# Three edits in a fused attention and token-MLP kernel: own buffers for the last residual, earlier operand sums, merged steps

## Chip, core and metric

The kernel runs on one core of one Trainium2 chip. The metric is device time of one execution in microseconds (us), lower is better. Engines are called PE (TensorE, matrix products), PEld (its weight loads), DVE (VectorE), ACT (ScalarE), POOL (GpSimd) and SP (SyncE, which here only issues transfers).

## What is computed

One block on x of 2048 tokens x 512 channels, in float32. First h = x + A(layernorm(x)), where A is a linear attention with 32 heads. Then

```
n = layernorm(layernorm(h))            # 2048 x 512
u = gelu(n^T @ w1 + b1)                # 512 x 1792, over the tokens
out = h + (u @ w2 + b2)^T              # 2048 x 512
```

The change lies in the second half, the two products with w1 (2048 x 1792) and w2 (1792 x 2048), which mix tokens.

## The kernel before

**Precision and products.** Every float32 operand is split into a high part (a copy rounded to the matmul's type, by ACT) and a low part (operand minus high part, by DVE or POOL), and a product is high x high + high x low + low x high: three matmuls. Both token products are done mostly by blocks of 2 x 2 tiles with seven block products instead of eight. That takes sums of tiles on both sides before the products, seven operands each, and sums of the seven results behind them. A tile is 128 x 128 on the weight's side and 128 x 256 (HD = 256 channels) on the other.

**w1 stage.** The 14 column tiles of w1 make 7 pairs p = 0 to 6. Pairs 0, 1, 2 and 6 are "plain pairs" (`fill`, or `seven_step` for the rest of pair 2): twelve matmuls of 512 columns for each two token tiles and pair of columns. Pairs 3, 4, 5 (`SEVEN`) go by seven products: 21 matmuls of 256 columns a step (L933). `RUN` lists the steps of the loop at L980: n = 0 to 5 are the last six steps of pair 2, n = 6 to 13 those of pair 3, 14 to 21 of pair 4, 22 to 29 of pair 5. In step n PE does the step, DVE makes the low part of step n + 1 (L912, or L914 in pair 2), a load is issued, DVE makes the weight sums of step n + 3 (L888 and L890, pairs 3 to 5 only) and ACT its high part (L894, or L884). The rings hold four raw tiles, three high and three low parts. `early` puts the gelu of pairs 0 and 1 and the last operand parts of h (`t_lo`, L647) into steps 0, 1 and 3. `seven_out` (L937) turns the seven results of a pair into u: it takes two places a step in the pair that follows. When pair p is done, `U[p]` holds gelu of its four tiles.

**Operands of u.** For the second product each pair needs three sums beside its four tiles, in a tile `tt`, and high and low parts of all seven. `near_ops` does it for pairs 0 and 1 into their own tiles `un`: the four sums on POOL (L807 to L810), the high parts on ACT (L816, L817), the low parts on DVE (L818, L819). Both pairs' `tt` come from the pool `ut`, which has one buffer. `near_ops(0)` is written into step 8 and `near_ops(1)` into step 16; their ACT and DVE parts follow two to five steps later through the lists `late` and `heavy`. `operands_u` (L821) does the same for pairs 2 to 6, the sums on DVE (L824 to L827) and the parts into `uf` tiles (ACT L61, DVE L62); there `tt` comes from `h7` for odd pairs and from `ut` for even ones. The buffer of `h7` first holds `hb7`, a part of h, whose last reader is `t_lo(7)` in step 3.

**w2 stage.** The steps are (sp, p), for eight token pairs sp and seven p; the weights come in groups of two steps (GRP = 2): load on SP (L1048), sums on DVE (L854 to L856), high part on ACT (L1066), low part on DVE (L1076). The first p of a token pair goes through `products`, the last two (last three for sp = 7) too, all at once. Those between go through `step`: five products as "wide" matmuls of 512 columns with the high weights (high and low of u side by side), then five of 256 columns with the low weights (L1104), then two products as six "narrow" ones (L1108). For sp = 7 all seven products are narrow, nine matmuls each for its last three p together, 63 in all. Behind each token pair DVE builds two output tiles in `ot` (one buffer, L1182 and `out_block`), and POOL's queue adds them to `out` in memory, which already holds h (L1169, L1175 to L1177). For the last token pair h is loaded instead (L1185, SP) into the same `ot`, b2 is added (L1186), and the results are added in place as the banks complete (L1187 to L1198): bank 0 after 18 of the 63 matmuls, bank 1 after 36, bank 2 after 54, bank 3 after the last. Three stores end the kernel (L1196, L1199).

**Order.** Inside `manual_schedule` the named engines take the instructions in the order of the text. What is outside (`operands_u`, the rest of pair 6, all of SP) is placed by the planner, which simulates the program and puts instructions where its simulation finds the engine free; it may put them between those of a manual order.

Of the kernel before, what the change touches and what calls it, by code (L numbers as in the profile page):

```python
# [9 lines left out]
F32 = mybir.dt.float32  # L10
# [7 lines left out]
P = 128  # L18
# [4 lines left out]
NP = NF // 2  # L23
HD = D // 2
GRP = 2
NG = 8
SEVEN = (3, 4, 5)
# [11 lines left out]
def block_kernel(ctx: ExitStack, tc: tile.TileContext, x, xT, wT, phic, wo, w1, b1, w2, b2,  # L39
# [753 lines left out]
    NEAR = 2  # L793
# [3 lines left out]
    def gelu(f, pu):  # L797
        if f % 2 == 0:
            U[f // 2] = ur.tile([P, 4, HD], F32, name="u")
        nc.scalar.activation(U[f // 2][:, f % 2 * 2:f % 2 * 2 + 2].rearrange("p k d -> p (k d)"), pu,  # L800
                             AF.Gelu_apprx_tanh, bias=b1s[:, f:f + 1])

    def near_ops(p):

        u = U[p]
        tt = ut.tile([P, 3, HD], F32, name="tt")
        nc.gpsimd.tensor_sub(tt[:, 0], u[:, 0], u[:, 1])  # L807
        nc.gpsimd.tensor_sub(u[:, 0], u[:, 2], u[:, 0])
        nc.gpsimd.tensor_sub(tt[:, 1], u[:, 2], tt[:, 0])
        nc.gpsimd.tensor_sub(tt[:, 2], u[:, 3], tt[:, 1])  # L810
        parts = [near[p][:, 0:4], near[p][:, 4:7]]
        for m in range(7):
            UB[p, m] = near[p][:, m]

        def high():
            nc.scalar.activation(parts[0][:, :, 0], u, AF.Copy)  # L816
            nc.scalar.activation(parts[1][:, :, 0], tt, AF.Copy)  # L817
        return [high, lambda: nc.vector.tensor_sub(parts[0][:, :, 1], u, parts[0][:, :, 0]),  # L818
                lambda: nc.vector.tensor_sub(parts[1][:, :, 1], tt, parts[1][:, :, 0])]  # L819

    def operands_u(p):  # L821
        u = U[p]
        tt = h7.tile([P, 3, HD], F32, name="tt", tag="h7") if p % 2 else ut.tile([P, 3, HD], F32, name="tt")
        nc.vector.tensor_sub(tt[:, 0], u[:, 0], u[:, 1])  # L824
        nc.vector.tensor_sub(u[:, 0], u[:, 2], u[:, 0])
        nc.vector.tensor_sub(tt[:, 1], u[:, 2], tt[:, 0])
        nc.vector.tensor_sub(tt[:, 2], u[:, 3], tt[:, 1])  # L827
        m = 0
        while m < 7:
            at = (p - NEAR) * 7 + m  # L830
            n = 2 if at % 2 == 0 and m not in (3, 6) else 1
            if at % 2 == 0:
                far[at // 2] = big.tile([P, 2, 2, HD], F32R, name="uf", tag="big")
            part = far[at // 2][:, at % 2:at % 2 + n]
            src = u[:, m:m + n] if m < 4 else tt[:, m - 4:m - 4 + n]
            split(part[:, :, 0], part[:, :, 1], src, nc.vector)
            for k in range(n):
                UB[p, m + k] = part[:, k]
            m += n
# [136 lines left out]
        return [lambda c=c: gelu(2 * p + c, PU[p][c]) for c in range(2)]  # L976

    early = {0: [*seven, *gelus(0)], 1: [lambda: t_lo(6), lambda: t_hi(7), *gelus(1)], 3: [lambda: t_lo(7)]}
    todo, heavy, late = [], [], []
    for n, (p, i) in enumerate(RUN):  # L980
        if n == NT // 2 - AHEAD:
            ms.close()
            ms.enter_context(tc.manual_schedule(engines={ET.PE, ET.DVE, ET.Activation, ET.Pool}))
        seven_step(p, i)
        seven_lo()
        seven_load()
        for op in early.get(n, []):
            op()
        if n == NT // 2 - AHEAD:
            for op in gelus(2):  # L990
                op()
        sum_with(*todo[:2])
        todo = todo[2:]
        if heavy:
            op = heavy.pop(0)
            op and op()
        if i == 1 and p > SEVEN[0]:
            todo += seven_out(p - 1)
        if i == 2 and 0 <= p - SEVEN[0] < NEAR:
            late = near_ops(p - SEVEN[0])  # L1000
        if i == 4 and late:
            late.pop(0)()
            heavy += [late[0], None, late[1]]
            late = []
    wst.close()
    hp = ctx.enter_context(tc.tile_pool(name="hp", bufs=1, reuse_waits="tile"))
    wst = ExitStack()
# [93 lines left out]
    def wide(sp, p, a, b, bk, low):  # L1101
        w, u = AW[sp, p][low][:, a], UB[p, b]
        o, u = (bank[bk][:, 0], u[:, 0]) if low else (bank[bk], u)
        nc.tensor.matmul(o, w, u, start=p == 0 and not low, stop=p == NP - 1, skip_group_check=True)  # L1104
# [3 lines left out]
            nc.tensor.matmul(bank[bk][:, half], AW[sp, p][x][:, a], UB[p, b][:, y], start=p == 0 and half == 0 and i == 0,  # L1108
                             stop=p == NP - 1 and i == 2, skip_group_check=True)

    def step(sp, p, order):
        for low in range(2):
            for a, b, bk, half in order:
                if half is None:
                    wide(sp, p, a, b, bk, low)
        for a, b, bk, half in order:
            if half is not None:
                narrow(sp, p, a, b, bk, half)

    def flat(a):  # L1120
        return a.rearrange("p k d -> p (k d)")
# [3 lines left out]
    for n, (sp, p) in enumerate(STEPS):  # L1125
        t = 2 * sp
        last = t + 2 == NT
        if n % GRP == 0 and p < NP - 1:
            lo_w2()
            hi_w2()  # L1130
            sums_w2()
        if p == 0:
            bank = []
            for _ in range(6):
                pool = (ps_f, ps_q, ps_b, ps_b)[n_bank % 8 // 2]
                bank.append(pool.tile([P, 2, HD], F32, name="py", tag="pu"))
                n_bank += 1
        order = LAST if last else PROD
        run_on = 3 if last else 2
        if p == 0:  # L1140
            products(sp, [p], order)
            continue
        if p < NP - run_on:
            step(sp, p, order)
            continue
        if p < NP - 1:
            continue
        products(sp, range(NP - run_on, NP), order)
        e = uo.tile([P, 2, HD], F32, name="e")
        u2 = uo.tile([P, HD], F32, name="u2", bufs=1)  # L1150
        u3 = uo.tile([P, HD], F32, name="u3")
        if not last:
            ot = uo.tile([P, 2, 2, HD], F32, name="ot", bufs=1)
            low = uo.tile([P, 3, HD], F32, name="low")
            nc.scalar.activation(e[:, 1], bank[0][:, 0], AF.Copy)
            for i in range(3):
                nc.scalar.activation(low[:, i], bank[3 + i][:, 1], AF.Copy)
            nc.vector.tensor_add(e[:, 1], bank[0][:, 1], e[:, 1])
            nc.vector.tensor_sub(u2, bank[1][:, 0], e[:, 1])
            nc.vector.tensor_add(u2, bank[1][:, 1], u2)  # L1160
            nc.vector.tensor_sub(u3, u2, bank[2][:, 0])
            nc.vector.scalar_tensor_tensor(e[:, 0], bank[2][:, 1], -1.0, u2, op0=ALU.mult, op1=ALU.subtract)

            def out_block(i, h, o, add):
                nc.vector.scalar_tensor_tensor(ot[:, i, h], o, b2s[:, t + i:t + i + 1], add, op0=ALU.add, op1=ALU.add)  # L1165

            out_block(0, 0, bank[2][:, 1], u3)
            out_block(0, 1, bank[3][:, 0], u3)
            nc.gpsimd.dma_start(out[t * P:(t + 1) * P, :], flat(ot[:, 0]), accum_op=ALU.add)  # L1169
            if n % GRP == 0:  # L1170
                lo_w2()
                hi_w2()
            out_block(1, 0, bank[4][:, 0], e[:, 0])
            out_block(1, 1, bank[5][:, 0], e[:, 1])
            nc.gpsimd.dma_start(out[(t + 1) * P:(t + 2) * P, :], flat(ot[:, 1]), accum_op=ALU.add)  # L1175
            nc.gpsimd.dma_start(out[t * P:(t + 1) * P, HD:D], low[:, 0], accum_op=ALU.add)
            nc.gpsimd.dma_start(out[(t + 1) * P:(t + 2) * P, :], flat(low[:, 1:3]), accum_op=ALU.add)  # L1177
            if n % GRP == 0:
                sums_w2()
            continue  # L1180

        ot = uo.tile([P, 2, 2, HD], F32, name="ot", bufs=1)  # L1182
        hb = [ot[:, i] for i in range(2)]
        for i in range(2):
            nc.sync.dma_start(flat(hb[i]), out[(t + i) * P:(t + i + 1) * P, :])  # L1185
            nc.vector.tensor_scalar(hb[i], hb[i], b2s[:, t + i:t + i + 1], None, op0=ALU.add)  # L1186
        nc.scalar.activation(e[:, 1], bank[0][:, 0], AF.Copy)  # L1187
        nc.vector.tensor_add(hb[1][:, 1], bank[0][:, 0], hb[1][:, 1])  # L1188
        nc.vector.tensor_sub(u2, bank[0][:, 1], e[:, 1])  # L1189
        nc.vector.tensor_sub(hb[1][:, 0], hb[1][:, 0], u2)  # L1190
        nc.vector.tensor_sub(u3, u2, bank[1][:, 0])  # L1191
        nc.vector.tensor_add(hb[0], hb[0], u3.unsqueeze(1).to_broadcast([P, 2, HD]))  # L1192
        nc.vector.tensor_add(hb[0][:, 0], bank[1][:, 1], hb[0][:, 0])  # L1193
        nc.vector.tensor_sub(hb[1][:, 0], hb[1][:, 0], bank[1][:, 1])  # L1194
        nc.vector.tensor_add(hb[0][:, 1], bank[2][:, 0], hb[0][:, 1])  # L1195
        nc.sync.dma_start(out[t * P:(t + 1) * P, :], flat(hb[0]))  # L1196
        for k, o, q in ((0, bank[2][:, 1], nc.scalar), (1, bank[3][:, 0], nc.sync)):
            nc.vector.tensor_add(hb[1][:, k], o, hb[1][:, k])  # L1198
            q.dma_start(out[(t + 1) * P:NT * P, k * HD:(k + 1) * HD], hb[1][:, k])  # L1199
# [49 lines left out]
```

## Time and profile before

| | us |
|---|---|
| median of 3 runs | 521.54 |
| lowest and highest | 521.18, 522.02 |
| profiled execution | 521.74 |
| its span in the profile | 520.0 |

The span runs from the first to the last instruction in the profile; 1.7 us of the profiled execution lie around it. The TensorE clock was granted in full throughout. A row of a timeline gives start and duration in us, engine, line of the kernel, operation, result<-operands, shapes, count, and in brackets the engine's idle time just before and what ended it. Of matmul rows the starts are to be compared: their ends overlap. A row of the windows gives busy time and count of each engine in a stretch. A row of a line's view gives count, durations in ns (lowest, median, highest), and the first and last start.

### The profile page before, as it was taken

Reading aid. Unit: us, or ns where it says so; the run is one execution under the profiler, and the core shown is the slowest. Engines: PE = TensorE matmul, PEld = TensorE weight load, DVE = VectorE, ACT = ScalarE, POOL = GpSimd, SP = SyncE. Lnnn points to the kernel's source line nnn. Section 1 sums busy time; section 2 is a strip of 40 time slices with the busy share of each in tenths; the row PEclk is TensorE's granted clock in tenths of the full one; section 3 lists DMA queues with packets and bytes.
Section 4 is the critical chain, followed back from the end, with each engine's and each line's share of the span. In section 5 each row is a group of like instructions: output and inputs, shape, how many; then the busy total and the mean of one; then the engine's idle time right before and its main releaser. Section 6 shows DMA issues by size and latency. Waiting matters only on the chain. (4 is left out here: it accounts for less than half of the span.)

```text
span 520.0 us, 9480 instructions
## 1 busy us (share of the span) xinstructions
PE 511.8 (98%) x3595; PEld 442.1 (85%) x3595; DVE 445.0 (86%) x789; ACT 296.6 (57%) x494; POOL 245.7 (47%) x188
## 2 busy tenths in 40 slices
PE   8999999999999999999999999999999999999996
PEld 8788888887877767887788999998889999999996
DVE  6893999986899998877787679998999888988984
ACT  6998943524246876668976443556654434434430
POOL 2589799885999999875533003000002112211220
PEclk9999999999999999999999999999999999999999
DMA  8744310000131234343413333346125688667653
GB/s 310 271 139 122 82 42 21 1 1 3 42 123 60 103 84 129 112 128 119 151 50 101 97 88 102 87 123 236 62 88 112 165 184 171 139 151 190 139 71 102
DMA packets 36300, 58.56 MB, mean 113 GB/s; under 512 B 3744, under 2 KB 19360, under 8 KB 36256
## 3 DMA queue, kind: packets, MB, share of 16 engines
q1 hardware_dynamic: 31648, 50.85, 30.6%
q0 software_dynamic: 4032, 6.42, 9.8%
q8 instruction: 28, 0.46, 0.4%
q10 hardware_dynamic: 576, 0.69, 0.4%
q14 instruction: 16, 0.13, 0.1%
HBM read 46.81 MB, written 11.14 MB: 111 GB/s over the span
## 5 line engine op out<-in xcount | busy, mean ns | idle before, releaser
L1066 ACT ACTIVATE whi<-wraw 128x1792 fp32r<-128x1792 f32 x28 | 47.6, 1701 | 42.5 <-DVE wraw L856 21.1
L1076 DVE TENSOR_TENSOR wlo<-wraw,whi 128x1792 fp32r<-128x1792 f32 x28 | 56.6, 2020 | 8.8 <-PE py L1108 7.5
L1169 POOL DMA_DIRECT2D out<-ot x7 | 6.2, 885 | 110.4 <-DVE ot L1165 110.4
L67 PE MATMUL pu<-hs,whi 128*128 128x512 f32 x128 | 50.3, 393 | 1.2 <-POOL hs L62 1.2
L1104 PE MATMUL py<-uf,whi 128*128 128x512 f32 x175 | 50.0, 395 | 0.4 <-DVE uf L62 0.4
L66 PE MATMUL pu<-hs,whi 128*128 128x512 f32 x128 | 50.1, 399 | 0.0
L68 PE MATMUL pu<-hs,wlo 128*128 128x512 f32 x128 | 48.3, 390 | 0.0
L894 ACT ACTIVATE whi<-wraw 128x896 fp32r<-128x896 f32 x24 | 22.9, 953 | 33.8 <-DVE wraw L890 18.6
L456 POOL TENSOR_TENSOR ez<-eq,zB 128x1024 f32<-128x1024 f32 x16 | 38.4, 2400 | 4.4 <-ACT zB L503 4.4
L1108 PE MATMUL py<-uf,whi 128*128 128x256 f32 x210 | 39.0, 283 | 0.0
L933 PE MATMUL pu<-ht,whi 128*128 128x256 f32 x192 | 35.6, 283 | 0.0
L208 POOL TENSOR_TENSOR pk<-pk,sk 128x1024 f32<-128x1024 f32 x16 | 30.9, 1940 | 7.3 <-DVE sk L207 7.2
L62 POOL TENSOR_TENSOR hs<-hb,hs 128x512 fp32r<-128x512 f32 x16 | 22.4, 1400 | 23.9 <-ACT hs L61 23.8
L550 ACT ACTIVATE pht<-tn 128x512 f32<-128x512 f32 x32 | 17.4, 595 | 28.4 <-PE tn L548 28.3
L474 POOL TENSOR_TENSOR eq<-eq,w 128x1024 f32<-128x1024 f32 x16 | 32.4, 2027 | 1.3 <-DVE w L471 1.2
L1108 PEld LDWEIGHTS py<-uf,whi 128*128 128x128 f32 x210 | 32.7, 192 | 0.0
L1104 PEld LDWEIGHTS py<-uf,wlo 128*128 128x128 f32 x175 | 28.5, 189 | 4.9
L1104 PEld LDWEIGHTS py<-uf,whi 128*128 128x128 f32 x175 | 29.2, 189 | 3.4 <-DVE uf L62 0.7
L212 POOL TENSOR_TENSOR zacc<-zacc,pk 128x1024 f32<-128x1024 f32 x13 | 31.3, 2405 | 0.5
L66 PEld LDWEIGHTS pu<-hs,whi 128*128 128x128 f32 x128 | 24.0, 188 | 7.1 <-issue 2.5
L933 PEld LDWEIGHTS pu<-ht,whi 128*128 128x128 f32 x192 | 29.9, 192 | 0.0
L912 DVE TENSOR_TENSOR wlo<-wraw,whi 128x896 fp32r<-128x896 f32 x24 | 26.0, 1085 | 4.5 <-ACT whi L894 4.5
(207 smaller groups left out, 1626.9 us busy)
## 6 DMA issues: line engine op xcount, KB each, us to landing
wraw<-in_w SPq DMA_DIRECT2D x28, 512.0 KB, 4.5
wraw<-in_w SPq DMA_DIRECT2D x48, 256.0 KB, 2.8
xraw<-in_xT SPq DMA_DIRECT2D x16, 256.0 KB, 3.1
xh<-in_x SPq DMA_DIRECT2D x16, 256.0 KB, 2.7
h<-in_x SPq DMA_DIRECT2D x16, 256.0 KB, 2.7
out<-h SPq DMA_DIRECT2D x14, 256.0 KB, 2.9
out<-ot POOLq DMA_DIRECT2D x14, 256.0 KB, 4.9
wraw<-in_wT SPq DMA_DIRECT2D x12, 256.0 KB, 4.9
```

Source lines behind the costliest of these rows:

```text
L66: nc.tensor.matmul(o, ah, bh, start=first, stop=False)
L67: nc.tensor.matmul(o, ah, bl, start=False, stop=False)
L68: nc.tensor.matmul(o, al, bh, start=False, stop=last)
L208: nc.gpsimd.tensor_mul(heads(PK[t]), heads(PK[t]), sk.unsqueeze(2).to_broadcast([P, 2 * H, DH]))
L212: nc.gpsimd.tensor_add(zacc, zacc, PK[t])
L456: nc.gpsimd.tensor_mul(EZ[t], EQ[t], zB)
L474: nc.gpsimd.tensor_mul(heads(EQ[t]), heads(EQ[t]), W[t].rearrange("p g c h -> p (g c h)").unsqueeze(2).to_broadcast([P, 2 * H, DH]))
L933: nc.tensor.matmul(ACC[p][bk][:, half], WS[p, i][x][:, a], hb[b][y], start=i == 0 and half == 0 and k == 0, stop=i == NT // 2 - 1 and k == ...
L1066: nc.scalar.activation(WH[g], RAW[g], AF.Copy)
L1076: nc.vector.tensor_sub(wl_, RAW[g], WH[g])
L1104: nc.tensor.matmul(o, w, u, start=p == 0 and not low, stop=p == NP - 1, skip_group_check=True)
L1108: nc.tensor.matmul(bank[bk][:, half], AW[sp, p][x][:, a], UB[p, b][:, y], start=p == 0 and half == 0 and i == 0, stop=p == NP - 1 and i == ...
```

## The change

Three edits. (1) `near_ops` takes `tt` as `operands_u` does, so pair 1 gets the buffer in `h7`; and its parts move in the loop: the POOL sums of pair 0 to step 1, those of pair 1 to step 4, and the ACT and DVE parts, three for each pair, to steps 2, 3, 4 and 6, 8, 10. (2) `step` becomes `steps`: two steps that use one weight group are done together, the wide high matmuls of both first, then the low and narrow ones of the first, then of the second. (3) For the last token pair the residual gets two tiles of its own, `hb0` and `hb1`, instead of `ot`.

```diff
+    def sums_tile(p):
+        return h7.tile([P, 3, HD], F32, name="tt", tag="h7") if p % 2 else ut.tile([P, 3, HD], F32, name="tt")
...
-        tt = ut.tile([P, 3, HD], F32, name="tt")
+        tt = sums_tile(p)
...
-    todo, heavy, late = [], [], []
+    todo, late = [], []
+    NEAR_AT, LATE_AT = (1, 4), (2, 3, 4, 6, 8, 10)
...
-        if heavy:
-            op = heavy.pop(0)
-            op and op()
         if i == 1 and p > SEVEN[0]:
             todo += seven_out(p - 1)
-        if i == 2 and 0 <= p - SEVEN[0] < NEAR:
-            late = near_ops(p - SEVEN[0])
-        if i == 4 and late:
+        if n in NEAR_AT:
+            late += near_ops(NEAR_AT.index(n))
+        if late and n in LATE_AT:
             late.pop(0)()
-            heavy += [late[0], None, late[1]]
-            late = []
...
-    def step(sp, p, order):
-        for low in range(2):
+    def steps(sp, ps, order):
+        for p in ps:
             for a, b, bk, half in order:
                 if half is None:
-                    wide(sp, p, a, b, bk, low)
-        for a, b, bk, half in order:
-            if half is not None:
-                narrow(sp, p, a, b, bk, half)
+                    wide(sp, p, a, b, bk, 0)
+        for p in ps:
+            for a, b, bk, half in order:
+                if half is None:
+                    wide(sp, p, a, b, bk, 1)
+            for a, b, bk, half in order:
+                if half is not None:
+                    narrow(sp, p, a, b, bk, half)
...
-            step(sp, p, order)
+            if n % GRP == 0 or p == 1:
+                steps(sp, range(p, min(p + GRP - n % GRP, NP - run_on)), order)
...
-        ot = uo.tile([P, 2, 2, HD], F32, name="ot", bufs=1)
-        hb = [ot[:, i] for i in range(2)]
+        hb = [uo.tile([P, 2, HD], F32, name=f"hb{i}", bufs=1) for i in range(2)]
```

More of the change, by code (lines that the diff above doesn't have):

```diff
@@ L822, in operands_u @@
         u = U[p]
-        tt = h7.tile([P, 3, HD], F32, name="tt", tag="h7") if p % 2 else ut.tile([P, 3, HD], F32, name="tt")
+        tt = sums_tile(p)
         nc.vector.tensor_sub(tt[:, 0], u[:, 0], u[:, 1])
```

## Prediction

> **What bounds the kernel now.** I began with the page: its first part says which engine fills the span.
>
> ```profile
> span 520.0 us, 9480 instructions
> PE 511.8 (98%) x3595; PEld 442.1 (85%) x3595; DVE 445.0 (86%) x789; ACT 296.6 (57%) x494; POOL 245.7 (47%) x188
> ```
>
> TensorE is busy for 98% of the span, and the change leaves the number and the shapes of its matmuls alone. So it can only win by closing holes in the PE row, or by shortening the tail that follows the last matmul; and it can lose by opening new ones. I looked for holes in the windows, in the stage whose matmuls are all alike (L933, 256 columns each).
>
> ```profile
> 300.00:320.00 20.00, 20.00 (x169) 20.00 (x168) 17.30 (x30) 9.24 (x11) 4.68 (x4) 1.00 0.33 94
> 320.00:340.00 20.00, 19.49 (x157) 18.73 (x156) 19.84 (x47) 9.71 (x12) 0.00 (x0) 1.00 0.33 93
> ```
>
> Columns: length, then busy us and count of PE, PEld, DVE, ACT and POOL, then the granted clock (1.00 in both). At the same clock the second 20 us hold 12 matmuls fewer, while DVE is busy for 19.84 of 20 with 47 instructions instead of 30. The timeline of PE shows such a hole, the view of line 933 who ended it:
>
> ```profile
> 335.62 0.28 PE L933 MATMUL pu<-hs,wlo 128*128 128x256 f32 x1
> 335.74 0.40 PE L933 MATMUL pu<-hs,whi 128*128 128x256 f32 x2
> 336.43 0.39 PE L933 MATMUL pu<-hs,wlo 128*128 128x256 f32 x1 [0.29 <-DVE wlo L912]
> ```
> ```profile
> L933 PE MATMUL pu<-hs,wlo x72: 283/283/387, 292.4 to 354.0; 128*128 128x256 f32 x72
>   DVE wlo L912: 1.8, 6
> ```
>
> Undisturbed starts lie 0.12 us apart (335.62 to 335.74). The stage has 24 steps of 21 matmuls, 504 in all; that row holds the stage's 3rd matmul (292.4) and its 504th (354.0). 501 x 0.12 = 60.1 us should lie between them; it is 61.6. **About 1.5 us** are lost, where PE waits for the low part of the w1 weights, which DVE makes. After this stage one more hole stands out:
>
> ```profile
> 389.90 0.50 PE L1104 MATMUL py<-uf,whi 128*128 128x512 f32 x1 [0.39 <-DVE uf L62]
> ```
>
> The end I read from the chain that ended last, then from the timelines of PE, ACT, DVE and SP.
>
> ```profile
> 502.91 5.32 DMA out<-ot
> ...
> 508.80 3.41 DMA ot<-out
> ...
> 514.40 0.70 DVE ot L1192
> ...
> 516.54 0.33 DVE ot L1198
> ```
> ```profile
> 509.84 0.28 PE L1108 MATMUL py<-uf,wlo 128*128 128x256 f32 x1
> ...
> 515.24 0.28 PE L1108 MATMUL py<-uf,wlo 128*128 128x256 f32 x1
> 510.16 0.38 ACT L1187 ACTIVATE e<-py 128x256 f32<-128x256 f32 x1 [6.14 <-PE py L1108]
> 516.13 0.74 DVE L1198 TENSOR_TENSOR ot<-py,ot 128x256 f32<-128x256 f32 x2
> 443.29 45.54 SPq L1048 DMA_DIRECT2D wraw<-in_w  x10
> ```
>
> No matmul stands in this chain: the store of the token pair before the last has to leave `ot`, then the residual is loaded into `ot`, then DVE works off its list, until 516.87, though the last matmul started at 515.24.
>
> **Part 1, own buffers for the residual.** The load no longer waits for `ot`. SP has issued its last weight load by 488.8 (443.29 + 45.54), ten in 45 us, so two more issues fit between them or behind them; the 3.4 us load and both L1186 are then over before bank 0 is ready. How soon after its last matmul a bank can be read: the 18th of the last 63 matmuls completes bank 0; it starts at 515.24 - 45 x 0.12 = 509.84, and ACT reads at 510.16, 0.32 later. By the same step bank 1 (36th) is ready at 512.3, bank 2 (54th) at 514.5, bank 3 (63rd) at 515.56. DVE keeps up with that: between banks 1 and 2 stand L1191 to L1194, three of 256 columns (0.34 each, as the chain's 0.33 for L1198) and L1192 with 0.70, 1.7 us of the 2.2; behind bank 2 L1195 and the first L1198, 0.7 us, until 515.2. The last L1198 then runs from 515.56 for 0.41, to 515.97 instead of 516.87: **-0.9 us**. How long the last store takes to land I leave as it is. Ends: 0 (the load still comes late) and -1.3 (the store also lands sooner, since the other two are out of its way; my estimate, no row shows it). I take -0.9, whose rows are this very stretch. What is late next is PE itself.
>
> **Part 2, sums of pairs 0 and 1 in the plain pairs.** The instructions are the same; those of L807 to L819 move from steps 8 to 21 to steps 1 to 10. Before, they lie thus (timelines of POOL, then DVE):
>
> ```profile
> 313.07 1.45 POOL L807 TENSOR_TENSOR tt<-u 128x256 f32<-128x256 f32 x1 [31.66 <-DVE un L819]
> ...
> 316.23 1.68 POOL L810 TENSOR_TENSOR tt<-u,tt 128x256 f32<-128x256 f32 x1
> ```
> ```profile
> 308.00 1.08 DVE L912 TENSOR_TENSOR wlo<-wraw,whi 128x896 fp32r<-128x896 f32 x1
> ...
> 309.98 1.08 DVE L912 TENSOR_TENSOR wlo<-wraw,whi 128x896 fp32r<-128x896 f32 x1
> ...
> 313.85 0.96 DVE L888 TENSOR_TENSOR wraw<-wraw 128x256 f32<-128x256 f32 x1
> 314.84 1.46 DVE L890 TENSOR_TENSOR wraw<-wraw 128x128 f32<-128x128 f32 x2
> ...
> 318.22 0.62 DVE L890 TENSOR_TENSOR wraw<-wraw 128x128 f32<-128x128 f32 x2
> ...
> 319.76 0.42 DVE L888 TENSOR_TENSOR wraw<-wraw 128x256 f32<-128x256 f32 x1
> ...
> 328.34 1.22 DVE L818 TENSOR_TENSOR un<-u,un 128x1024 fp32r<-128x1024 f32 x1
> ...
> 330.81 0.42 DVE L824 TENSOR_TENSOR tt<-u 128x256 f32<-128x256 f32 x1
> ...
> 334.42 0.95 DVE L819 TENSOR_TENSOR un<-tt,un 128x768 fp32r<-128x768 f32 x1
> ...
> 336.63 0.42 DVE L824 TENSOR_TENSOR tt<-u 128x256 f32<-128x256 f32 x1
> ```
>
> Pair 1's sums on POOL waited 31.66 us for the one buffer of `tt` and fell into pair 4's steps. A step of seven products costs DVE 1.98 us (308.00 to 309.98) and PE 21 x 0.12 = 2.52: DVE has 0.54 to spare, 4.3 in the eight steps of pair 4. What they, and the first of pair 5, had to take besides: L818 and L819 of pair 1, 2.2; the seven operations of `seven_out`, 0.34 each, 2.4; L824 to L827 of pairs 3 and 2, eight of the same size, 2.7; and the slowing of DVE while POOL summed, 0.54 on an L888 (0.96 for 0.42) and 0.84 on the L890 (1.46 for 0.62), 1.4. That is 8.7 against 4.3. The ring of three high parts lets DVE be some 3 us late: a slot comes free when PE ends step n, ACT's copy and DVE's subtraction take 2.1, and PE reaches step n + 3 two steps, 5.04, later. 8.7 - 4.3 - 3 = 1.4, close to the 1.5 that PE lost. After the change the 2.2 and the 1.4 are gone from here. 2.4 + 2.7 = 5.1 stay (3.7 if the planner takes pair 2's four earlier, whose `tt` is free from step 4 on), against 4.3 + 3: no wait. **-1.5 us**; ends 0 (the lateness shows up elsewhere) and -1.5 (no more is lost there).
>
> Where they go there must be room (timelines of DVE, ACT and PE):
>
> ```profile
> 282.62 1.22 DVE L647 TENSOR_TENSOR ht<-hb,ht 128x1024 fp32r<-128x1024 f32 x1
> 284.06 0.63 ACT L884 ACTIVATE whi<-wraw 128x512 fp32r<-128x512 f32 x1 [2.09 <-PE pu L67]
> 305.78 1.04 ACT L816 ACTIVATE un<-u 128x1024 fp32r<-128x1024 f32 x1
> 289.48 0.39 PE L66 MATMUL pu<-hs,whi 128*128 128x512 f32 x1
> 292.43 0.28 PE L933 MATMUL pu<-hs,wlo 128*128 128x256 f32 x1
> ```
>
> Pair 1's `tt` now takes the buffer of `hb7`, whose last reader is this L647; so POOL starts at 283.84 and needs 4.8 us (313.07 to 317.91 above). DVE from there on, in its order: the sums of step 6, slowed by POOL as above, until 286.2; L818 of pair 0, whose high part ACT makes behind this L884, 284.7 + 1.0, so no wait; the low part of step 5, done at 288.0 and needed by step 5's third matmul, 289.48 + 2 x 0.23 = 289.9; the sums of step 7, slowed by another 0.54; L819; the low part of step 6, done at 291.4 and needed at 292.43. Queued behind L818 on DVE are exactly these, and PE waits for none: 1.9 and 1.0 us to spare. I take 0; the other end is the lock among the rivals. Pair 1's own L818 and L819, 2.2 us in steps 8 and 10, meet 0.54 of room in every step from 6 to 13, and their readers come in the last stage, after all of L933: covered.
>
> The slow L888 are a lock at work. The Trainium skill, page "SBUF — State Buffer", section "Who interferes with whom", says that a DVE instruction with two SBUF inputs and a GpSimd instruction that reads SBUF shut each other out, and that the first holds the port for its whole length. The trace agrees: 0.42 becomes 0.96, and L810 takes 1.68 beside an L912. By that rule alone DVE could stand still for POOL's whole 4.8 us; the low part of step 5 would then come 1.1 late, that of step 6 another 0.4, and the sum would be 520.7.
>
> **Part 3, merged steps.** For each two steps merged, the second's five wide high products come 16 matmuls earlier, and the first's low and narrow ones 5 x 0.23 = 1.2 us later.
>
> ```profile
> 398.99 1.32 PE L1104 MATMUL py<-uf,whi 128*128 128x512 f32 x5
> 400.15 0.76 PE L1104 MATMUL py<-uf,wlo 128*128 128x256 f32 x5
> ```
>
> Five wide ones take 1.16, 0.23 each as between the L66 of the plain pairs, and 256 columns take 0.12 wherever they stand; a new order of the same shapes changes no pace that I can read. A weight set's last use stays where it was, so no buffer comes free later. The 1.2 us of grace for the low weights would pay only where PE waits for them, and past 391 I found no such wait. **0**; ends -0.1 and +0.1 (0.01 us of pace, the last digit of these rows, at each of the ten merges).
>
> **Sum.** The profiled execution took 521.74 (its span of 520.0 and 1.7 around it). 521.74 - 0.9 - 1.5 = 519.3; the median of the runs, 521.54, lies 0.2 lower than that execution: **519.2**.
>
> **Rivals.** Two rows first, of the windows and of DVE's timeline:
>
> ```profile
> 360.00:380.00 20.00, 20.00 (x97) 16.66 (x96) 19.96 (x40) 13.52 (x22) 0.00 (x0) 1.00 0.25 82
> ```
> ```profile
> 354.28 0.69 DVE L665 TENSOR_TENSOR wlo<-wlo,whi 128x512 fp32r<-128x512 f32 x1 [1.83 <-PE pu L933]
> ```
>
> - *Given back* (520.7): behind the seven-product stage DVE has hardly a gap (first row below, 19.96 of 20), and its last `uf` already holds PE up at 389.90. If that date stays, PE waits there for the 1.5. Against it: this work begins behind PE's last L933 (second row: 1.83 of DVE's idle time end there), so it should move as a whole. 0.15.
> - *Load still late* (520.1): the planner puts the residual's load last on SP, or its new place in memory is free late. Against it: only weight loads stand on that queue. 0.09.
> - *Lock in the plain pairs* (522.6, slower): after 283.84 pair 1's sums on POOL shut DVE out. Were all four as long as the longest, 4 x 1.68 = 6.7, the low part of step 5 would be done at 292.9, 3.0 late, that of step 6 another 0.4: 3.4 lost for 2.4 gained. It decides from 5.8 us of standstill on (0.9 less than 6.7 takes 0.9 off the 3.4); 1.4 was measured. 0.12.
> - *More goes* (518.6): the hole at 389.90 closes as well. 0.08.
>
> **How the numbers follow.** The forecast has 0.56, with 518.8 to 519.9 as its own range. A measurement of this kernel tells 0.2%, 1.04 us, from no change. Faster: forecast, late load and more, 0.73. Same: given back, and the milder locks (0.05), 0.20. Slower: 0.07. The range, 518.4 to 521.1, takes in all but the worse locks and the edges of the others.
>
> **What would show it.** Right: no wait of L933 for L912; L807's second run near 284; `hb` loaded before 505; the last L1198 starting within 0.4 us of the last matmul. Wrong: PE waiting for L914 or L912 between 286 and 296, a longer wait at the first use of pair 6's operands, or a `hb` load in the last 12 us.

## The result and the profile after

| | before | after |
|---|---|---|
| median | 521.60 us (4 runs, 521.18 to 522.02) | 519.34 us (4 runs, 518.96 to 519.63) |
| ratio | | 0.9956 (95%: 0.9939 to 0.9973) |
| profiled execution | 521.74 us | 518.96 us |
| its span | 520.0 us | 516.9 us |

The forecast was 519.2. By the medians the change gains 2.3 us, by the two profiled executions 3.1 us of span. The lines of the changed kernel lie up to three further on, or one back: L933 is now L936, L912 L915, L888 L891, L890 L893, L818 L821, L819 L822, L824 L827, L1104 L1103, L1108 L1107, L1198 L1201. In the page and the windows of the changed kernel (columns as before) PE has filled up:

```profile
span 516.9 us, 9476 instructions
PE 510.2 (99%) x3595; PEld 441.9 (85%) x3595; DVE 444.8 (86%) x789; ACT 296.9 (57%) x494; POOL 244.9 (47%) x188
```
```profile
320.00:340.00 20.00, 20.00 (x169) 20.00 (x168) 18.16 (x44) 9.06 (x11) 0.00 (x0) 1.00 0.38 106
```

169 matmuls start in these 20 us instead of 157. The view of line 936 has the seven-product stage from end to end:

```profile
L936 PE MATMUL pu<-hs,whi x144: 278/283/284, 292.0 to 352.3; 128*128 128x256 f32 x144
...
L936 PE MATMUL pu<-hs,wlo x72: 283/283/284, 292.3 to 352.4; 128*128 128x256 f32 x72
its engine sat idle before it (us, times) until:
who waited for it (us, times):
  ACT whi L897: 27.7, 19
...
```

Nobody is named under "sat idle until". From the first matmul's start to the last one's are 60.35 us, 503 x 0.12; before it was 61.82. Now ACT waits 19 times for PE to free a high part (before, 6 times): the ring is full, as it should be where PE is the limit. The sums of pair 1 lie where they were meant to (POOL's timeline, then DVE's beside it):

```profile
283.80 0.79 POOL L810 TENSOR_TENSOR tt<-u 128x256 f32<-128x256 f32 x1 [2.57 <-PE pu L67]
...
286.24 1.60 POOL L813 TENSOR_TENSOR tt<-u,tt 128x256 f32<-128x256 f32 x1
```
```profile
284.03 1.53 DVE L893 TENSOR_TENSOR wraw<-wraw 128x128 f32<-128x128 f32 x2
285.50 1.74 DVE L821 TENSOR_TENSOR un<-u,un 128x1024 fp32r<-128x1024 f32 x1
287.16 1.22 DVE L917 TENSOR_TENSOR wlo<-wraw,whi 128x512 fp32r<-128x512 f32 x1
...
290.16 1.08 DVE L915 TENSOR_TENSOR wlo<-wraw,whi 128x896 fp32r<-128x896 f32 x1
...
293.04 0.42 DVE L827 TENSOR_TENSOR tt<-u 128x256 f32<-128x256 f32 x1
```

While POOL sums, L893, L821 and L917 take 0.91, 0.52 and 0.53 longer than elsewhere, 2.0 us together; the low part of step 6 is done at 291.24 all the same, 1.0 before PE needs it. Pair 0's sums on POOL have hardly moved: they begin at 276.62 before and at 276.45 now, and wait for the gelu of pair 0 (L800) both times. Pair 2's sums have moved forward by themselves, from 336.63 to 293.04: their buffer is free. The hole at pair 6's first use has moved by 1.65 us and kept its size:

```profile
388.25 0.50 PE L1103 MATMUL py<-uf,whi 128*128 128x512 f32 x1 [0.41 <-DVE uf L62]
```

At the end PE now leads (timelines of PE, DVE and SP):

```profile
513.36 0.28 PE L1107 MATMUL py<-uf,wlo 128*128 128x256 f32 x1
512.94 0.41 DVE L1201 TENSOR_TENSOR hb<-py,hb 128x256 f32<-128x256 f32 x1
513.67 0.42 DVE L1201 TENSOR_TENSOR hb<-py,hb 128x256 f32<-128x256 f32 x1 [0.32 <-PE py L1107]
375.64 0.90 SPq L1188 DMA_DIRECT2D hb<-out  x2
514.12 0.34 SPq L1202 DMA_DIRECT2D out<-hb  x1
```

The residual was loaded at 375.64. The last add starts 0.31 us behind the last matmul; from that matmul's start to the end of the span are 3.5 us, where it was 4.7 (515.24 to 519.97). I call this stretch the tail below.

Where the 3.1 us of span went: 0.17 came before the first edit (the stage's first matmul starts at 292.02 for 292.20, and PE's 301st matmul is already as much earlier, 51.59 for 51.75), 1.47 in the seven-product stage, 0.23 between it and the last matmul (160.98 us for 161.21), 1.2 in the tail. The first of these is not the change's: it differs as much between executions of one kernel.

### The profile page after: what moved, and what is told of

Read it like the earlier page. It is cut to its first block, busy times and chain, and to the rows that moved or that the text cites. A ratio compares the mean times of both kernels' runs of the same rounds, so it can differ in the third digit from the quotient of the medians.

```text
span 516.9 us, 9476 instructions
## 1 busy us (share of the span) xinstructions
PE 510.2 (99%) x3595; PEld 441.9 (85%) x3595; DVE 444.8 (86%) x789; ACT 296.9 (57%) x494; POOL 244.9 (47%) x188
## 4 chain that ended last, share of the span: by engine, by line
PE 86%; POOL 7%; DVE 3%; ACT 1%; issue 1%; DMA 1%; POOLq 0%
PE py L1103 15%; PE pu L936 12%; PE py L1107 10%; PE pu L66 7%; PE pu L67 7%; PE pu L68 7%; PE pv L67 3%; PE pv L68 3%; PE pv L66 3%; PE pk_ps L66 2%; PE pk_ps L67 2%; PE pk_ps L68 2%; POOL ez L456 2%; POOL eq L474 2%; PE po L68 2%; PE tn L548 2%
## 5 line engine op out<-in xcount | busy, mean ns | idle before, releaser
L1103 PE MATMUL py<-uf,whi 128*128 128x512 f32 x175 | 48.7, 394 | 0.4 <-DVE uf L62 0.4
L1107 PE MATMUL py<-uf,whi 128*128 128x256 f32 x210 | 39.0, 283 | 0.0
L936 PE MATMUL pu<-ht,whi 128*128 128x256 f32 x192 | 35.6, 283 | 0.0
L62 POOL TENSOR_TENSOR hs<-hb,hs 128x512 fp32r<-128x512 f32 x16 | 22.4, 1399 | 23.9 <-ACT hs L61 23.8
L1103 PEld LDWEIGHTS py<-uf,whi 128*128 128x128 f32 x175 | 29.8, 189 | 4.2 <-DVE uf L62 0.7
L1107 PEld LDWEIGHTS py<-uf,whi 128*128 128x128 f32 x210 | 32.7, 192 | 0.0
L1103 PEld LDWEIGHTS py<-uf,wlo 128*128 128x128 f32 x175 | 27.9, 190 | 4.0
L936 PEld LDWEIGHTS pu<-ht,whi 128*128 128x128 f32 x192 | 30.0, 192 | 0.0
L1107 PE MATMUL py<-uf,wlo 128*128 128x256 f32 x105 | 29.7, 283 | 0.0
```

Of the source, the lines that this page charges most:

```text
L936: nc.tensor.matmul(ACC[p][bk][:, half], WS[p, i][x][:, a], hb[b][y], start=i == 0 and half == 0 and k == 0, stop=i == NT // 2 - 1 and k == ...
```

## Experiments

Two lengths are read from each trace beside the time: the seven-product stage (first to last of its 504 matmuls; 60.35 is without loss) and the tail. The two profiled executions of the changed kernel differ by 0.8 us in when this stage begins (292.02 and 292.79), so these lengths are sharper than the totals. One more length is used, the slowing: by how much the DVE operations that run while POOL sums pair 1 are longer than others of their line and shape, added up. "Before" is the kernel before on the same chip.

### Each part alone

The residual's tiles alone:

```diff
-        ot = uo.tile([P, 2, 2, HD], F32, name="ot", bufs=1)
-        hb = [ot[:, i] for i in range(2)]
+        hb = [uo.tile([P, 2, HD], F32, name=f"hb{i}", bufs=1) for i in range(2)]
```

> The kernel before with the last residual in tiles of its own and nothing else. The prediction's part 1 says that PE's row stays as it was (last matmul near 515.2) and that the last DVE add ends 0.9 us earlier; the trace after the whole change shows a tail (last matmul's start to the end of the span) of 3.5 us for 4.7, so 1.2 us in all: 520.4. Rival, load still late: tail 4.7 and 521.6. Rival, the other 0.3 us of the shorter tail belong to another edit: tail 3.8 and 520.7.

520.24 against 521.25, ratio 0.9982 (0.9973 to 0.9991). Stage 61.83, last matmul 514.97, tail 3.49. So this edit alone gives the short tail. But the five kernels below that keep the old `ot` have tails of 3.87 to 4.17, not 4.7; the chain of the one with merged steps alone shows why:

```profile
502.68 4.94 DMA out<-ot
...
508.19 3.31 DMA ot<-out
```

Its store out of `ot` lands at 507.62, 7.6 us before its last matmul (515.19); in the profiled execution of the kernel before it was 508.23, 7.0 us before the last matmul. Everything behind it hangs on that landing and on the load that follows, so the old tail changes with them, and the new one doesn't: 3.49 to 3.50 in all six traces with `hb`. The tail has two parts. From the last matmul's start to the end of the last add it is 0.8 to 1.6 in the six traces with the old `ot` and 0.74 in the six with `hb`; from there to the end of the span it is 3.08 or 3.09 in the former and 2.75 or 2.76 in the latter. So 0.33 us of the gain is the end of the last store coming sooner, in every trace; why it does, no run here tells.

The sums in the plain pairs alone (buffer and steps):

> The kernel before with the sums of pairs 0 and 1 in the plain pairs (buffer and steps) and nothing else. Part 2 says that the seven-product stage, 61.8 us from first to last matmul's start before, takes 60.4 (503 x 0.12), that everything behind it comes 1.5 us earlier and that the tail stays 4.7: 520.1. Rival, given back: the stage takes 60.4, but PE's wait at the first use of pair 6's operands grows from 0.55 to 2 us: 521.6.

519.71 against 521.25, 0.9974 (0.9963 to 0.9986). Stage 60.35; at pair 6's first use PE loses 0.56 against its pace (0.39 of it idle), for 0.55 before. Nothing is given back.

The merged steps alone:

> The kernel before with merged steps and nothing else. The prediction says 0 within 0.1 us: 521.6. Rival, read from the trace after the whole change, where the stretch behind the last wait is 0.23 us shorter: ten merges save some 0.02 us each, last matmul near 515.0 and 521.4. Nothing else in the trace should change.

521.02 against 521.25, ratio 1.0 (0.9991 to 1.0009): no difference that the time can show. The trace is finer: stage 61.84 as before, but from its end to the last matmul 160.99 us, against 161.21 before and 161.18, 161.17 and 161.15 in the three kernels beside it without merged steps (the residual's tiles, the sums, the buffer). It is the rival's 0.2, or 0.02 at each of ten merges. PE's timeline of this kernel has ten wide matmuls in 2.29 us,

```profile
381.18 2.46 PE L1104 MATMUL py<-uf,whi 128*128 128x512 f32 x10
383.47 0.76 PE L1104 MATMUL py<-uf,wlo 128*128 128x256 f32 x5
```

where twice five took 2 x 1.16. Why the longer run goes a little faster for each matmul, these rows don't tell.

### The buffer without the new steps

Only `sums_tile` and its use in `near_ops`:

```diff
...
     def near_ops(p):
         u = U[p]
-        tt = ut.tile([P, 3, HD], F32, name="tt")
+        tt = sums_tile(p)
```

> The kernel before with a buffer of its own for pair 1's sums, but the old steps: the POOL sums run near 284 instead of 313, while the ACT and DVE parts of pair 1 stay in steps 18 to 21. If the slowing of DVE by POOL in pair 4 is a term of its own as large as the prediction has it (1.4 us), the lateness falls from 8.7 - 7.3 to 7.3 - 7.3, and the stage's loss from 1.5 to 0 to 0.3: 520.3. Rival, only DVE's own 2.2 us in pair 4 count: the loss stays near 1.5 and the time near 521.6.

519.58 against 521.25, 0.9965 (0.9952 to 0.9979). The stage has no loss: first matmul at 291.94, last at 352.30, and L821 and L822 of pair 1 still run at 327.13 and 332.25. The few lines of the buffer do all that part 2 does. Its DVE and POOL timelines show two things at once:

```profile
283.72 0.79 POOL L810 TENSOR_TENSOR tt<-u 128x256 f32<-128x256 f32 x1 [2.56 <-PE pu L67]
```
```profile
313.93 0.42 DVE L827 TENSOR_TENSOR tt<-u 128x256 f32<-128x256 f32 x1
...
327.13 1.22 DVE L821 TENSOR_TENSOR un<-u,un 128x1024 fp32r<-128x1024 f32 x1
...
334.45 0.42 DVE L827 TENSOR_TENSOR tt<-u 128x256 f32<-128x256 f32 x1
```

POOL's sums have left pair 4, and pair 2's sums on DVE, which waited for the same buffer, now come at 313.93, early in pair 4, instead of at 336.63. Either could be the cause; the next two kernels tell them apart.

### POOL's sums put back into pair 4, and more of them

With the buffer, POOL is held until pair 4 by three small operations on 16 columns, so that only its sums go back (`gate` is a tile of 16 columns; the lines of the buffer are those above):

```diff
...
+            if p == 4:
+                seen = WS[RUN[n + 2]][0]
+                nc.gpsimd.tensor_sub(gate, seen[:, 1, :16], seen[:, 2, :16])
+                nc.gpsimd.tensor_sub(U[1][:, 0, :16], U[1][:, 0, :16], gate)
+                nc.gpsimd.tensor_add(U[1][:, 0, :16], U[1][:, 0, :16], gate)
             late = near_ops(p - SEVEN[0])
```

> The kernel with the buffer of its own for pair 1's sums and the old steps, but POOL has to wait for a weight tile of pair 4 before it sums (three small POOL operations on 16 columns, which subtract a number from u and add it again, so these columns are rounded once more). So the sums lie in pair 4 again, while pair 2's sums on DVE stay where the freed buffer put them, in step 14. Theory, POOL's slowing is a term of its own: loss 1.0 to 1.9 us again, time 1.0 to 1.9 above the kernel with the buffer alone. Rival, what counted was that pair 2's sums moved to step 14: loss below 0.3.

520.82 against 521.45, 0.9990 (0.9981 to 0.9999). Stage 61.37, loss 1.02; POOL and DVE of this kernel:

```profile
319.02 0.81 POOL L810 TENSOR_TENSOR tt<-u 128x256 f32<-128x256 f32 x1
...
321.47 1.47 POOL L813 TENSOR_TENSOR tt<-u,tt 128x256 f32<-128x256 f32 x1
```
```profile
319.61 0.37 DVE L893 TENSOR_TENSOR wraw<-wraw 128x128 f32<-128x128 f32 x1
319.90 0.41 DVE L954 TENSOR_TENSOR u<-pu,u 128x256 f32<-128x256 f32 x1
320.24 0.56 DVE L893 TENSOR_TENSOR wraw<-wraw 128x128 f32<-128x128 f32 x1
320.71 1.63 DVE L915 TENSOR_TENSOR wlo<-wraw,whi 128x896 fp32r<-128x896 f32 x1
322.26 0.95 DVE L891 TENSOR_TENSOR wraw<-wraw 128x256 f32<-128x256 f32 x1
```

With pair 2's sums left where the freed buffer puts them (314.14), POOL's presence alone brings two thirds of the loss back. The other third is 0.46, and the slowing accounts for it. Here it is 0.54 and 0.53 on L915 and L891 and 0.09 and 0.27 on the two single L893 (0.29 or 0.28 elsewhere), 1.4 together; L954, which reads one operand from a matmul's result `pu`, is not longer beside POOL. In the kernel before it is 1.9: to the slow rows of the prediction comes one more, the first below (the others are used at the end):

```profile
317.23 0.96 DVE L888 TENSOR_TENSOR wraw<-wraw 128x256 f32<-128x256 f32 x1
...
321.34 1.08 DVE L912 TENSOR_TENSOR wlo<-wraw,whi 128x896 fp32r<-128x896 f32 x1
...
323.74 1.08 DVE L912 TENSOR_TENSOR wlo<-wraw,whi 128x896 fp32r<-128x896 f32 x1
...
338.04 1.08 DVE L912 TENSOR_TENSOR wlo<-wraw,whi 128x896 fp32r<-128x896 f32 x1
```

So it is 0.5 us smaller here, and the loss is 0.46 smaller. Nothing is left for the place of pair 2's sums. The three small operations themselves slow DVE by no more than 0.02 on any row.

The kernel before, with pair 1's fourth sum five times over:

```diff
-        nc.gpsimd.tensor_sub(tt[:, 2], u[:, 3], tt[:, 1])
+        for _ in range(5 if p else 1):
+            nc.gpsimd.tensor_sub(tt[:, 2], u[:, 3], tt[:, 1])
```

> The kernel before, where pair 1's fourth sum on POOL is made five times over (the same value each time), so four more POOL operations of 256 columns run in pair 4's steps. If POOL's sums slow DVE there as the prediction's part 2 has it (1.4 us for four of them, up to 1.9 with the third slow row), the stage's loss grows from 1.5 to 2.9 to 3.4 us and the time by 1.4 to 1.9. Rival, the slowing costs PE nothing and only DVE's own work counts: loss 1.5, time as before.

522.98 against 521.45, 1.0027 (1.0017 to 1.0037). Stage 63.32, loss 2.97; the view of its line 934 puts it down to the low part again (L913 here), and DVE's timeline has the slow rows:

```profile
  DVE wlo L913: 4.2, 10
```
```profile
314.38 0.97 DVE L889 TENSOR_TENSOR wraw<-wraw 128x256 f32<-128x256 f32 x1
315.38 1.45 DVE L891 TENSOR_TENSOR wraw<-wraw 128x128 f32<-128x128 f32 x2
...
317.76 0.95 DVE L889 TENSOR_TENSOR wraw<-wraw 128x256 f32<-128x256 f32 x1
318.75 1.52 DVE L891 TENSOR_TENSOR wraw<-wraw 128x128 f32<-128x128 f32 x2
...
321.19 0.95 DVE L889 TENSOR_TENSOR wraw<-wraw 128x256 f32<-128x256 f32 x1
...
322.40 0.49 DVE L891 TENSOR_TENSOR wraw<-wraw 128x128 f32<-128x128 f32 x1
```

Four more sums on an engine that is idle there cost PE 1.5 us. The slowing is 3.6, so in four kernels PE's loss follows it: 0, 1.4, 1.9 and 3.6 of slowing in pair 4 go with losses of 0, 1.0, 1.5 and 3.0.

### More sums in the plain pairs

The same edit in the changed kernel, to see how much room the new place has:

> The changed kernel, where pair 1's fourth sum is made five times over, now in the plain pairs: POOL works from 284 to some 292 instead of 288. In the changed kernel the low part of step 6 is done 1.0 us before PE needs it. Theory, each four POOL sums cost DVE 1.4 to 1.9 us: PE waits for 0.4 to 0.9 us at steps 6 or 7, and the ring takes the rest. The rival of the prediction, DVE stands still while POOL works: the low part comes some 4 us later and 3 us or more are lost. Third: DVE catches up within the spare time, nothing is lost.

520.33 against 521.45, 0.9979 (0.9970 to 0.9988). Stage 61.49, loss 1.14, in one hole (timelines of POOL, DVE and PE of this kernel):

```profile
286.81 6.05 POOL L814 TENSOR_TENSOR tt<-u,tt 128x256 f32<-128x256 f32 x5
```
```profile
288.89 0.95 DVE L892 TENSOR_TENSOR wraw<-wraw 128x256 f32<-128x256 f32 x1
289.87 1.53 DVE L894 TENSOR_TENSOR wraw<-wraw 128x128 f32<-128x128 f32 x2
...
292.19 1.62 DVE L916 TENSOR_TENSOR wlo<-wraw,whi 128x896 fp32r<-128x896 f32 x1
```
```profile
293.87 0.39 PE L937 MATMUL pu<-hs,wlo 128*128 128x256 f32 x1 [0.88 <-DVE wlo L916]
```

The three DVE rows are 0.53, 0.91 and 0.54 longer than their like: 2.0 us for four sums more, 0.5 each. The spare time of 1.0 us was real, and it was all there was: 2.0 - 1.0 is nearly the 1.14 lost. DVE doesn't stand still while POOL works. The two take turns, and POOL pays too: five sums take 6.05 us, where one takes 0.74 while DVE is idle (L810 at 280.67 in the kernel before). The exclusion that the Trainium skill describes ("SBUF — State Buffer", section "Who interferes with whom") fits these rows; my reading of it as a standstill for POOL's whole stretch does not.

### The old steps, and one more line

The changed kernel with the old steps, and the changed kernel again beside it:

> The changed kernel with the old steps for the parts of pairs 0 and 1 (8 to 21), so with pair 1's own buffer, the merged steps and the residual's tiles. If the buffer alone took away the 1.5 us, as the kernel with the buffer alone says, the stage takes 60.4 us and the time is the changed kernel's within 0.2 us: 519.2. Rival, the new steps have a share: the stage takes 60.6 or more.

> The changed kernel as it is, beside the one with the old steps on the same chip: 519.2, stage 60.4 us, tail 3.5 us again. If the tail is now set by PE's last matmul alone, it is 3.5 in this execution too, whatever the landing time of the stores before.

518.91 and 519.68 (before: 521.35), ratios 0.9959 (0.9946 to 0.9972) and 0.9967 (0.9955 to 0.9979). Both have a stage of 60.35 and tails of 3.49 and 3.50. In the two profiled executions the stage began at 292.15 and 292.79, and that is the difference between their spans (516.98 and 517.64); it stands already at PE's 301st matmul (51.71 and 52.39), long before any step that differs. So the new steps bring nothing that these times can show. What they change is the spare time. The tightest low part of the stage with the old steps is that of step 24 (DVE, then PE's third matmul of that step):

```profile
336.06 1.09 DVE L915 TENSOR_TENSOR wlo<-wraw,whi 128x896 fp32r<-128x896 f32 x1
```
```profile
337.74 0.28 PE L936 MATMUL pu<-hs,wlo 128*128 128x256 f32 x1
```

It is done 0.59 before PE needs it. With the new steps no low part of pairs 4 and 5 is done less than 1.7 ahead, but that of step 6 is only 1.0 ahead.

One wait was left in the last stage, for pair 6's operands. They are asked for later if pair 5 joins pair 4 in a step:

```diff
-        run_on = 3 if last else 2
+        run_on = 3 if last else 2 if sp else 1
```

> The changed kernel, where for the first token pair only pair 6 goes through the products at the end; pair 5 is merged with pair 4 in a step. Pair 6's operands are then needed 2.5 us later than now. Expected: the 0.58 us that PE waits for them at 387.4 go, all behind comes 0.6 us earlier: ratio to the changed kernel 0.999. Rival: the seven results of the first token pair are now all made within 2.5 us instead of 5, DVE and ACT empty the banks too late, and PE waits for a bank in the second token pair, for as much or more.

518.47 against 521.45, 0.9943 (0.9930 to 0.9955): the lowest ratio of all, though its interval overlaps with those of the changed kernel, which did not run beside it. The trace is clearer. PE's waits name no L62 any more, and from the stage's end to the last matmul are 160.35 us, against 160.98. Its PE and DVE at the place:

```profile
389.35 0.40 PE L1103 MATMUL py<-uf,whi 128*128 128x512 f32 x1
389.58 0.28 PE L1103 MATMUL py<-uf,wlo 128*128 128x256 f32 x1
...
391.83 0.40 PE L1103 MATMUL py<-un,whi 128*128 128x512 f32 x1
```
```profile
387.65 1.02 DVE L62 TENSOR_TENSOR uf<-tt,uf 128x512 fp32r<-128x512 f32 x2
```

The operands are ready at 388.67, pair 6 begins at 389.35, and the next token pair follows at 391.83 without a wait for a bank.

## Why the prediction was right, point by point

- **Part 1, -0.9 us.** The mechanism is as described: the load comes early, PE is late next, and the last add starts 0.31 us behind the last matmul for the 0.32 assumed. The add ends 0.90 nearer to the last matmul, as forecast. But the term was mis-sized in two ways. The end of the last store also comes 0.33 sooner: the end of -1.3 that I had not taken was the nearer one, 1.2 against the profiled execution. And that execution's tail of 4.73 is the longest of six: against the five other traces with the old `ot` the gain is 0.4 to 0.7, of which 0.33 is the store's and only 0.04 to 0.34 that of the earlier load. The timed difference, 0.0018 x 521.25 = 0.9 (0.5 to 1.4), doesn't decide between them. So the agreement with -0.9 is in part luck.
- **Part 2, -1.5 us.** It is 1.47, at the place named: PE waits for the low part no more, and nothing is given back at pair 6, whose hole kept its size. That DVE's load in pair 4 is the cause, with POOL's slowing as a term of its own, held in all three cases tried: without it no loss, with it in pair 4 again 1.0, with twice as many sums 3.0. What I overlooked: by the same sum (8.7 against 7.3), taking POOL's term away was enough, so the new steps had nothing left to do. I gave the gain to the whole edit and not to the buffer.
- **The terms of that sum.** That 8.7 - 4.3 - 3 came so near to the loss is luck. POOL's slowing is 1.9 and not 1.4, because I missed the slow L888 at 317.23. The lead was 1.5 and not 3 when pair 4 began (the low part of step 14 is done at 311.06, and PE needs it at 312.59), since DVE was still making pair 0's low parts; one of these, at 311.98, is not in the sum. Against that, the last late low part is that of step 24, at 338.04, so the room is that of ten steps, 5.4 and not 4.3; and two operations of `seven_out` in between the weight sums of a step cost 0.42 together, not 0.68 (the L912 at 321.34 and 323.74 are 2.40 apart for 1.98). By the rows, from 309.98 to 338.04 are 28.06 us, which is ten steps of 1.98 and 8.3 more: 8.3 - 5.4 - 1.5 = 1.4.
- **Room in the plain pairs.** The low part of step 6 is done at 291.2; the forecast was 291.4, and PE needs it at 292.3. I had slowed the weight sums by POOL's presence, but not L821 and L917. The total came out all the same (2.0 for 1.9): the size was right and the places were not.
- **Part 3, 0.** The step that failed is "a new order of the same shapes changes no pace that I can read": it is 0.02 us a merge, 0.2 in all, twice the end that I had set. It doesn't show in the time.
- **The total.** By the medians it is 2.3 for a forecast of 2.4. With a tail like that of the other traces the parts are 1.5, 0.2 and 0.4 to 0.7: a smaller part 1 and an unforeseen part 3 made up for each other.
- **The rivals.** Given back: refuted. Load still late: refuted. Lock in the plain pairs: the lock is there, at 0.5 us a sum instead of the whole stretch; my price was for a standstill that doesn't happen. More goes: not by this change, but by one line more.

## What to carry to other kernels

An engine that is idle can still slow its neighbour, so where a buffer makes work wait on an idle engine, look at what it will run beside when it is let go; here the wait of 31.7 us on POOL looked harmless and its end cost 1.5 us of PE. Sum up the fullest engine's load by stage against its room plus the ring's lead: here that sum would have told which half of an edit was needed. Read the lead from the rows where the stage begins, and count every slowed row; a sum that comes out right can still have its terms wrong. A tail that hangs on a queue's landing varied from 3.9 to 4.7 us in six traces; with a buffer of its own for the last load it was 3.5 in six.

## What the runs showed that I had not expected

- One POOL sum of two tiles of 256 columns costs DVE about 0.5 us if DVE works on operations with two inputs in SBUF beside it, and costs POOL about as much (1.2 us for 0.74). DVE operations with one input in a matmul's result (L953 and L954 of the kernel with late sums) were not slowed (0.42 and 0.41).
- Wide matmuls in one run of ten start 0.229 us apart (2.29 / 10), in runs of five 0.232 (1.16 / 5).
- The old tail took 4.73, 4.17, 4.06 and 3.96 us in the kernel before and in those with the buffer, the merged steps and the sums alone, and 3.87 in both with more or late sums in pair 4. In the same order the store out of `ot` landed 7.0, 7.4, 7.6, 7.8, 7.9 and 7.6 us before the last matmul, and the load into `ot` behind it 3.0, 3.6, 3.7, 3.8, 3.9 and 3.9: this lead and the tail add up to 7.75 or 7.76 in all six.
